# Four heads at a time through a block-causal attention in front of a two-layer network

## The chip, the cores and the metric

The kernel runs on one core of one Trainium2 chip, in one launch. The core has a matrix engine (TensorE; PE in the profile, its weight loads PEld), a vector engine (VectorE, DVE), a scalar engine (ScalarE, ACT), a general engine (GpSimd, POOL) and a sync engine (SyncE, SP) whose queue issues nearly all transfers. The metric is device time in microseconds. Times of one kernel are given as the median of several runs; a profile is one execution.

## The reference

The attention has 8 batches of 8 heads, 576 positions and 64 values per head. A query sees all keys of its own block of 64 positions and of earlier blocks. Its output is laid out as 4608 tokens of 512 values and goes through a network with a hidden layer of 2048 and a leaky activation with one slope per hidden unit. Everything is float32.

```python
scores = scale * np.matmul(q, k.transpose(0, 1, 3, 2))       # scale = 1/8
mask = block_i >= block_j                                    # blocks of 64 positions, 9 of them
scores = np.where(mask, scores, -1000000000.0)
scores = scores - np.max(scores, axis=-1, keepdims=True)
attn = np.exp(scores)
attn = attn / (np.sum(attn, axis=-1, keepdims=True) + 1e-09)
out = np.matmul(attn, v)
x = out.transpose(0, 2, 1, 3).reshape(B * S, H * D)
h = x @ w_in
g = np.maximum(h, 0.0) + alpha * np.minimum(h, 0.0)
y = g @ w_out
```

## The kernel before

The work has two stages that overlap. In the first, the attention runs pair of heads by pair of heads (32 pairs), and beside it the part of the network that belongs to the first 6 of 16 hidden blocks (`FA`) is computed for chunks of 256 tokens (`chunk_a`, 18 chunks: `ffn1` at L501, `activate`, `ffn2` at L540). Its results go to memory (`part`). In the second stage the other 10 hidden blocks are computed for chunks of 512 tokens (`pair1`, L581, with fewer products by a Strassen scheme, and `ffn2`), and the partial sums are added. Weights arrive as 64-bit numbers and are made float32 by seven instructions (`to_f32`, 512 columns at a time, a "piece"), and each operand of the dense products is split into a rounded high part and a low part (`split`).

All instructions are given to a planner (`Plan`) with a cost and a priority. The planner simulates the engines greedily and writes out one order for each engine; on the chip each engine runs its order and waits where data are late. What the simulation takes as cost (`c_tiled` and others) decides only about order. Buffers are taken by the planner too: three "duos" (two PSUM banks each) serve the attention, two more banks the dense products.

One pair of heads in the attention has these steps. Score products (`scores`, L722, K=64 rows by 32 columns of weights) put a block of 64 queries onto 128 partitions, `32*i`: `i // 2` chooses the half of the queries and `i % 2` the half of each key block, so that one query's keys lie in two partition rows and one query block `T` needs `32 * (T + 1)` columns. The blocks of a pair go in three sets: TOP (8, 6), MID (7, 5), LOW (4 to 0). DVE takes row maxima (L727), POOL exchanges them between the two rows of a query (`swap`, L699, four copies), DVE combines them (L730), ACT takes exponentials and row sums (L735, an activation and a reading of the accumulator each), and DVE transposes 32x32 blocks (L739) into `PTL` (query blocks 0 to 3) and `PTH` (4 to 8). `factors_of` exchanges the sums (L699 again), inverts them (L750) and spreads them over the partitions (L756 on ACT, L758 on DVE). `values` (L780, 64x64 products) multiplies with the values: for each key block `j`, two heads `h` and two query halves `g`, with all query blocks that see it as columns. One instruction of DVE (L786) multiplies by the inverse sums and writes `xT`, a ring for two batches in SBUF. A float32 matmul that the kernel writes appears in the trace as two matmul records.

The first four query blocks of a batch are computed a batch ahead of the others (`SKEW`): the four pairs of batch 0 start with FIRST (3 to 0) alone, and the last four pairs have no LOW set but THEN (4,). After each batch `spill` writes its part of `xT` to memory (`xd`) for the second stage, and `chunk_x` takes 256 tokens from the ring, splits them and starts a chunk; `tail_x` collects the last 64 tokens of four batches. Four weight pieces of the second stage are converted during the attention and stored (`AHEAD`, `weights_ahead`, `wd`); the others are converted when the attention has ended.

Of the kernel before, what the change touches and what calls it, by code (L numbers as in the profile page):

```python
# [29 lines left out]
RING = 2 * S  # L30
# [9 lines left out]
LAG = 6.25  # L40
VL = 1.0
E0, E1 = -5, 1
NEAR = 20
FP = -1
AHEAD = {(8 + k // 2, k % 2): 12 + 4 * k for k in range(4)}
# [5 lines left out]
RB, EB, EF = 2, 3, 4  # L51
LO_A = ("POOL", "POOL")
QA, VA = 3, 3
PB, QB, VB, TB, CB = 5, 3, 3, 2, 6
SWAP = "POOL"
RCP = ("ACT", "ACT", "ACT", "ACT")
PM, PX, PT, PZ, PU = -7, -8, -1, -1, -10
GH, XH, XC = ("ACT", "POOL"), "ACT", 2
LATER = ("DVE", "POOL", "DVE", "POOL", "DVE", "DVE")
# [5 lines left out]
TO_POOL = 85  # L65


IN_ORDER = {"q", "k", "v", "p", "PTL", "PTH", "z", "r", "R", "raw", "m", "ef", "xb", "X", "xt", "qa", "va", "tail"}
# [16 lines left out]
class Plan:  # L85
# [44 lines left out]
    def schedule(self):  # L130
# [43 lines left out]
        while events:  # L174
# [13 lines left out]
            for engine, heap in ready.items():  # L188
# [29 lines left out]
                if engine == "PE":  # L218
                    saved = SWITCH if before and before.tiled and cost.tiled else 0.0
                    before = cost  # L220
                    cost = clock(t, cost) - saved
                elif engine in ("DVE", "ACT", "POOL"):
                    cost *= LONGER
# [31 lines left out]
    def issue(self):  # L255
        for _, i in self.schedule():
            self.ops[i][2]()

# [42 lines left out]
def attn_ffn(ctx, tc, qT, kT, vT, w_in, w_out, alpha, out):  # L301
# [26 lines left out]
    xT = xring.tile([P, NCC, RING], F32, name="xT")  # L328
# [12 lines left out]
    def rooms(pool, *kinds):  # L341
        for kind, n, shape, dt in kinds:
# [4 lines left out]
    rooms(st, ("q", QB, [S - CHA], F32), ("qa", QA, [2, CHA], F32), ("va", VA, [4, 2, D], F32), ("k", QB, [S], F32), ("v", VB, [NT, 2, D], F32), ("p", PB, [1024], F32),  # L347
          ("PTL", TB, [1024], F32), ("PTH", TB, [2880], F32), ("c", CB, [3, 10], F32), ("z", 2, [3, 2 * NT], F32),
          ("r", 2, [2, NT], F32), ("R", 2, [2, 32 * NT], F32))
    rooms(xring, ("tail", 1, [NCC, CHA], F32), ("xh", XC, [NCC, CHA], F32R), ("xl", XC, [NCC, CHA], F32R))  # L350
# [15 lines left out]
    def to_f32(src, prio, after=(), early=None):  # L366
# [17 lines left out]
        op("DVE", 350, lambda: nc.vector.tensor_scalar(  # L384
# [4 lines left out]
        op("DVE", 390, lambda: nc.vector.tensor_scalar(  # L389
            out=fr(), in0=high(), scalar1=0xFFFFF, scalar2=0x100000, op0=ALU.bitwise_and, op1=ALU.bitwise_or),  # L390
            r=[raw], w=[eb], prio=prio)
        op("DVE", 760, lambda: nc.vector.scalar_tensor_tensor(  # L392
# [3 lines left out]
        op("DVE", 680, lambda: nc.vector.scalar_tensor_tensor(  # L396
# [5 lines left out]
    def split(src, hi, lo, n, r, hk, lk, claim, on, prio):  # L402

        op("ACT", c_act(n, True), lambda: nc.scalar.copy(out=hi(), in_=src()), r=r, w=[hk], claim=claim, prio=prio)  # L404
        op(on, c_pool(n) + 60 if on == "POOL" else 1.4 * c_dve(n), lambda: (nc.gpsimd if on == "POOL" else nc.vector).tensor_tensor(  # L405
            out=lo(), in0=src(), in1=hi().bitcast(F32), op=ALU.subtract), r=[*r, hk], w=[lk], claim=claim, prio=prio)
# [12 lines left out]
    def add(e, n, to, a, b, f, prio, r=()):  # L419

        op(e, c_pool(n) if e == "POOL" else 1.3 * c_dve(n), lambda: (nc.gpsimd if e == "POOL" else nc.vector).tensor_tensor(
# [4 lines left out]
    def weights_ahead(p):  # L426

        for f, i in (k for k in AHEAD if AHEAD[k] == p):
            pr = 5 * p + 100
            mb, _ = to_f32((w_in, w_out)[i][f].bitcast(I32), pr, [("x", p // NP % 2, p % NP, 1)])  # L430
# [116 lines left out]
    def factors(t0):  # L547
# [3 lines left out]
           r=["att", *[("xd", b, i) for b in range(t0 // S, (t0 + CHB - 1) // S + 1) for i in range(2)]], w=[xb], prio=0 if t0 else XB)  # L551
# [76 lines left out]
    def chunk_x(b, part, s0):  # L628

        xh, xl = Buf("xh"), Buf("xl")  # L630
        r0 = b % 2 * S + s0
        split_x(lambda: xT[:, :, r0:r0 + CHA], xh, xl, slice(0, CHA), xs(b, (part,)), 0, FP, CHA)
        return xh, xl, [0]

    tails = {}

    def tail_x(b):

        i = b % (CHA // 64)
# [18 lines left out]
    def blocks(ap, n, j0):  # L658

        return ap[:, :64 * n].rearrange("p (j x) -> p j x", x=64)[:, :, j0:j0 + 32]  # L660

    def prep(p, pr):

        q, k, v = Buf("q"), Buf("k"), Buf("v")
        op("SP", 160, lambda: nc.sync.dma_start(out=q(), in_=qT[p, :, CHA:]), w=[q], prio=pr)
        op("SP", 288, lambda: nc.sync.dma_start(out=k(), in_=kT[p]), w=[k], prio=pr)
        op("SP", 576, lambda: nc.sync.dma_start(out=v(), in_=vT[p]), w=[v], prio=pr + VL)
        return (lambda: q(), lambda: k(), CHA, [q, k]), v

    def prep_first(p, pr):  # L670

        qk, v = Buf("qa"), Buf("va")
        for i, src in enumerate((qT, kT)):
            queue, issuer = (("SP", nc.sync), ("ACTQ", nc.scalar))[i and not p]
            op(queue, 128, lambda i=i, src=src, issuer=issuer: issuer.dma_start(out=qk()[:, i], in_=src[p, :, :CHA]), w=[(qk, i)], prio=pr)
        op("SP", 256, lambda: nc.sync.dma_start(out=v(), in_=vT[p, :, :4]), w=[v], prio=pr + VL)
        return (lambda: qk()[:, 0], lambda: qk()[:, 1], 0, [(qk, 0), (qk, 1)]), v

    def at_T(T):

        u = T - 4 if T > 3 else T
        return 32 * u * (18 if T > 3 else 8)

    def run_of(T, T1, h, j):

        u, step = (T - 4, 18 + h) if T > 3 else (T, 8 + h)
        start = step * u + h * (5 if T > 3 else 1) + j
        return start, step, T1 - T

    def swap(t, to, of, n, keys, key, scale, pr):  # L690

        cost = {"DVE": 75, "POOL": 258, "ACT": 150}[SWAP]

        def move(a, b):
            o, i = t()[a, to, n], t()[b, of, n]
            if SWAP == "ACT":
                nc.scalar.activation(out=o, in_=i, func=AF.Copy, scale=scale)
            else:
                (nc.vector if SWAP == "DVE" else nc.gpsimd).tensor_scalar(out=o, in0=i, scalar1=scale, scalar2=None, op0=ALU.mult)  # L699
        for i in range(4):  # L700
            a, b = slice(32 * i, 32 * i + 32), slice(32 * (i ^ 1), 32 * (i ^ 1) + 32)
            op(SWAP, cost, lambda a=a, b=b: move(a, b), r=keys, w=[(*key, i)], prio=pr)
        return [*keys, *[(*key, i) for i in range(4)]]

    def scores(src, Ts, pts, z, pr):

        sb, pb, c = Buf("duo"), Buf("p"), Buf("c")
        n = 2 * len(Ts)
        off, at = {}, 0
        for T in Ts:  # L710
            off[T] = at
            at += 32 * (T + 1)

        def qk_run():
            for T in Ts:
                w = 32 * (T + 1)
                q, k, q0, _ = src[T > 3]
                for i in range(4):
                    for h in range(2):
                        at = 64 * T - q0 + 32 * (i // 2)  # L720
                        hs, qs = slice(64 * h, 64 * h + 64), slice(at, at + 32)
# [207 lines left out]
```

## Time and profile before

| | |
|---|---|
| median of 3 runs | 1066.98 us (1065.96 to 1069.24) |
| the profiled execution | 1068.6 us, its span 1066.8 us |
| PE busy | 1013.9 us, 95% |
| DVE, ACT, POOL busy | 766.7, 590.7, 581.7 us |
| mean granted TensorE clock | 0.979 of full speed |
| DMA | 119.56 MB, 112 GB/s on average |

Views used below: the page gives busy shares; a table of stretches gives for each engine the busy microseconds and, in brackets, the number of instructions; a timeline gives start, length, engine, line, tiles and count of merged instructions, and in square brackets the idle time before them with what ended it ("issue": nothing that the profile shows). A group of instructions has, after the bar, busy time, mean nanoseconds of one, idle time before and its releaser.

### The profile page before, as it was taken

What the parts mean: (1) busy time and instruction counts of PE and PEld (TensorE: products, weight loads), DVE (VectorE), ACT (ScalarE), POOL (GpSimd) and SP (SyncE); (2) the same over time, 40 slices, a digit from 0 to 9 for tenths busy, and PEclk for the clock granted to TensorE, in tenths of its full rate; (3) what the DMA queues carried; (4) which work ended last, traced back from release to release, by engine and by line L of the source; (5) the groups of instructions that cost most, each with busy time, mean ns of one, the idle gap of its engine ahead of it and who ended that gap; (6) DMA issues with size and microseconds to landing.
All of it is one profiled execution on the core that took longest, in us unless ns stands there. A gap on an engine that the chain in (4) does not pass through costs nothing.

```text
span 1066.8 us, 32551 instructions
## 1 busy us (share of the span) xinstructions
PE 1013.9 (95%) x12860; PEld 876.9 (82%) x12860; DVE 766.7 (72%) x1674; ACT 590.7 (55%) x2106; POOL 581.7 (55%) x1036
## 2 busy tenths in 40 slices
PE   6667999999999999999998999999999999999998
PEld 4445888888888888888776879898989889898987
DVE  6899888878788877875889986656565556565552
ACT  6776868677766756865555553434343434343431
POOL 4778645564654654666999682525252525252521
PEclk9768999999999999999999999999999999999999
DMA  8534554453646354330633122121212121212021
GB/s 293 191 123 148 187 195 140 150 175 131 206 151 209 98 184 151 103 121 25 204 119 124 55 80 80 40 79 41 80 40 80 41 80 40 80 41 79 2 80 40
DMA packets 66890, 119.56 MB, mean 112 GB/s; under 512 B 10288, under 2 KB 31024, under 8 KB 66736
## 3 DMA queue, kind: packets, MB, share of 16 engines
q1 hardware_dynamic: 66304, 117.20, 33.1%
q8 instruction: 101, 1.65, 0.7%
q14 instruction: 53, 0.43, 0.1%
q10 hardware_dynamic: 432, 0.27, 0.1%
HBM read 87.04 MB, written 29.36 MB: 109 GB/s over the span
## 4 chain that ended last, share of the span: by engine, by line
PE 83%; DVE 6%; POOL 5%; issue 3%; ACT 3%; DMA 0%; SPq 0%; DVEq 0%; POOLq 0%; ACTq 0%
PE bank L540 34%; PE bank L581 19%; PE bank L501 14%; PE duo L722 8%; PE duo L780 8%; ACT p L735 2%; POOL gl L523 2%; POOL c L699 1%; DVE g L514 1%; DVE c L727 1%; DVE m L396 1%; DVE m L384 1%; DVE ef L389 1%; DVE ef L392 1%; DVE bank L594 0%
## 5 line engine op out<-in xcount | busy, mean ns | idle before, releaser
L523 POOL TENSOR_TENSOR gl<-g,gh 128x256 fp32r<-128x256 f32 x288 | 232.6, 811 | 284.1 <-ACT gh L520 268.7
L581 PEld LDWEIGHTS bank<-X,w 128*128 128x128 f32 x1890 | 254.4, 189 | 27.5 <-DVE X L405 2.7
L581 PE MATMUL bank<-X,w 128*128 128x256 f32 x1890 | 261.3, 282 | 7.0 <-DVE X L405 2.2
L735 ACT ACTIVATE p<-duo,c 128x256 f32<-128x256 f32 (+8 forms) x576 | 220.2, 413 | 47.1 <-DVE c L730 46.6
L540 PE MATMUL bank<-w,gh 128*128 128x512 f32 x720 | 225.4, 394 | 0.0
L512 ACT ACTIVATE g<-bank 128x256 f32<-128x256 f32 x288 | 109.0, 386 | 143.0 <-DVE bank L594 93.4
L514 DVE SCALAR_TENSOR_TENSOR g<-g,oal,bank 128x256 f32<-128x256 f32 x288 | 134.0, 474 | 42.5 <-ACT g L512 38.3
L520 ACT CAST gh<-g 128x256 fp32r<-128x256 f32 x234 | 94.6, 407 | 123.9 <-PE bank L540 98.3
L699 POOL TENSOR_SCALAR c<-c 32x4 f32<-32x4 f32 (+3 forms) x400 | 99.7, 249 | 100.9 <-DVE c L727 69.8
L594 DVE TENSOR_TENSOR bank<-bank,g 128x256 f32<-128x256 f32 x180 | 74.8, 427 | 109.8 <-PE bank L581 108.9
L540 PE MATMUL bank<-wa,gh 128*128 128x512 f32 x432 | 142.5, 410 | 8.9 <-ACT wa L404 3.2
L540 PE MATMUL bank<-w,gl 128*128 128x512 f32 x360 | 141.9, 394 | 0.0
L727 DVE TENSOR_REDUCE c<-duo 128x2 f32<-128x512 f32 (+8 forms) x288 | 123.8, 478 | 18.0 <-PE duo L722 17.6
L540 PEld LDWEIGHTS bank<-w,gh 128*128 128x128 f32 x720 | 121.2, 188 | 13.6
L735 ACT ACTIVATION_READ_ACCUMULATOR p<-duo,c 128x1 f32 x576 | 129.7, 225 | 0.0
L501 PE MATMUL bank<-xh,wa 128*128 128x256 f32 x864 | 127.6, 289 | 0.3 <-POOL wa L405 0.2
L501 PEld LDWEIGHTS bank<-xh,wa 128*128 128x128 f32 x864 | 113.6, 192 | 11.2 <-issue 6.1
L739 DVE STREAM_TRANSPOSE PTH<-p 128x576 f32<-128x576 f32 (+4 forms) x160 | 99.5, 630 | 16.2 <-ACT p L735 14.4
L540 PEld LDWEIGHTS bank<-wa,gh 128*128 128x128 f32 x432 | 78.1, 191 | 32.5 <-issue 5.6
L722 PE MATMUL duo<-k,q 64*32 64x288 f32 (+4 forms) x2560 | 85.1, 377 | 12.4 <-ACT p L735 12.3
L540 PE MATMUL bank<-wa,gl 128*128 128x512 f32 x216 | 88.0, 408 | 5.7 <-POOL gl L523 5.6
L590 DVE TENSOR_TENSOR g<-bank,g 128x256 f32<-128x256 f32 x135 | 55.9, 419 | 39.3 <-PE bank L581 39.2
(66 smaller groups left out, 1350.8 us busy)
## 6 DMA issues: line engine op xcount, KB each, us to landing
v<-in_v SPq DMA_DIRECT2D x32, 576.0 KB, 3.9
k<-in_k SPq DMA_DIRECT2D x32, 288.0 KB, 4.7
xb<-xd SPq DMA_DIRECT2D x9, 1024.0 KB, 5.4
m<-part SPq DMA_DIRECT2D x36, 256.0 KB, 3.5
out<-m SPq DMA_DIRECT2D x35, 256.0 KB, 2.0
va<-in_v SPq DMA_DIRECT2D x32, 256.0 KB, 4.5
raw<-in_w_in SPq DMA_DIRECT2D x16, 512.0 KB, 3.9
raw<-in_w_out SPq DMA_DIRECT2D x16, 512.0 KB, 3.5
```

What stands on the lines that cost most here:

```text
L501: nc.tensor.matmul(hp()[:, :n], ww()[:, 0, cc * P:(cc + 1) * P], x()[:, cc, :n], start=(i == 0 and cc == 0), stop=(i == 2 and cc == NCC - 1))
L512: op("ACT", c_act(CHA), lambda: nc.scalar.activation(out=g(), in_=hp()[:, ts], func=AF.Relu, scale=-1.0), r=[hp], w=[g], prio=FP)
L514: op("DVE", c_dve(CHA) + 60, lambda: nc.vector.scalar_tensor_tensor(out=g(), in0=g(), scalar=oal[:, f:f + 1], in1=hp()[:, ts], op0=ALU.mul ...
L520: op("ACT", c_act(CHA, True), lambda: nc.scalar.copy(out=gh(), in_=g()), r=[g], w=[gh], prio=FP)
L523: op("POOL", c_pool(CHA) + 60, lambda: nc.gpsimd.tensor_tensor(out=gl(), in0=g(), in1=gh().bitcast(F32), op=ALU.subtract), r=[g, gh], w=[g ...
L540: nc.tensor.matmul(acc(), a()[:, ts], ww(), start=(first and i == 0), stop=(last and i == 2))
L581: nc.tensor.matmul(bank()[:, :CHA], W()[:, i, 256 * at + P * c:256 * at + P * c + P], B()[:, j, CHA * c:CHA * c + CHA], start=(n == 0), st ...
L699: (nc.vector if SWAP == "DVE" else nc.gpsimd).tensor_scalar(out=o, in0=i, scalar1=scale, scalar2=None, op0=ALU.mult)
L722: nc.tensor.matmul(sb()[32 * i:32 * i + 32, h, off[T]:off[T] + w], q()[hs, qs], blocks(k()[hs], T + 1, 32 * (i % 2)), start=True, stop=True)
L727: op("DVE", c_dve(2 * w), lambda t=t, w=w, o=o: nc.vector.tensor_reduce(out=c()[:, 0, 2 * t:2 * t + 2], in_=sb()[:, :, o:o + w], axis=AX.X ...
L735: op("ACT", 237 + w / 1.2, lambda x=2 * t + h, T=T, h=h, w=w, o=o: nc.scalar.activation(out=pb()[:, 2 * o + h * w:2 * o + h * w + w], in_= ...
L739: op("DVE", 85 + 2.08 * w, lambda to=to, a=a, w=w, o=o: nc.vector.transpose(out=to()[:, a:a + 2 * w], in_=pb()[:, 2 * o:2 * o + 2 * w]), r ...
```

## The change

Four heads (two pairs) go through the attention together. The partition group `32*i` now holds pair `i // 2` and query half `i % 2`, so all keys of a query lie in one row, a query block needs `64 * (T + 1)` columns, and maxima and sums need no exchange: `swap` is gone. Block 8 has 576 columns and is cut into 512 and 64; its smaller maximum is taken from both cuts, and its sums are added. The three sets of two pairs become six sets of four heads. The transposed blocks now have 32 keys on the partitions of each pair and query half, so `values` multiplies 32 rows by 64 columns of weights: 32-key blocks `j` (two per key block), two heads `h` and four partition groups `i`, for three groups of query blocks (0 to 3, 4 to 6, 7 and 8) instead of two, into two duos at once.

x has no ring any more. The product with the inverse sums goes into a small tile `xo` for each pair and from there to memory at once; each chunk (`chunk_again`) loads its 256 tokens from `xd` again, all but the first chunk, which is taken from SBUF. The inverse sums are spread by 16 copies instead of 4, half on POOL and half on ACT. Sixteen weight pieces instead of four are converted ahead. The `gh` casts of the chunks all go to POOL, the low parts of later weights all to DVE, and most priorities and buffer numbers, and some of the costs that the planner uses, are set anew. q, k and v are loaded for four heads at once.

```diff
-TOP, MID, LOW = (8, 6), (7, 5), (4, 3, 2, 1, 0)
-FIRST, THEN = (3, 2, 1, 0), (4,)
+NQ = NPAIR // 2
+NB = NP // 2
+WHOLE = {T: (T, 0, 2 * T + 2) for T in range(NT)}
+LONG = ((8, 0, 16),), ((8, 16, 18), WHOLE[6]), (WHOLE[7],)
+BOTH = *LONG, (WHOLE[5], WHOLE[1]), (WHOLE[4], WHOLE[2]), (WHOLE[3], WHOLE[0])
+LAST = *LONG, (WHOLE[5],), (WHOLE[4],)
+FIRST = (WHOLE[3], WHOLE[2]), (WHOLE[1], WHOLE[0])
+GROUPS = (0, 4, 12, 52), (4, 7, 24, 76), (7, 9, 32, 68)
-C0, C1 = -3, 1.5
+C0, C1 = -3, 3.5
-AHEAD = {(8 + k // 2, k % 2): 12 + 4 * k for k in range(4)}
+AHEAD = {(8, 0): 3, (8, 1): 3, (9, 0): 4, ... (15, 0): 13, (15, 1): 14}
-GH, XH, XC = ("ACT", "POOL"), "ACT", 2
-LATER = ("DVE", "POOL", "DVE", "POOL", "DVE", "DVE")
+GH, XH, XC = ("POOL",), "ACT", 2
+LATER = ("DVE", "DVE", "DVE", "DVE", "DVE", "DVE")
...
+    def chunk_again(parts):
+        x = Buf("xc")
+        n = CHA // len(parts)
+        for i, (b, part, s0) in enumerate(parts):
+            op("SP", 2 * n, lambda i=i, b=b, s0=s0: nc.sync.dma_start(out=x()[:, :, n * i:n * i + n], in_=xd[:, :, b * S + s0:b * S + s0 + n]),
+               r=[("xd", b, part, pair) for pair in range(NP)], w=[(x, i)], prio=FP)
+        return chunk_x(x, [(x, i) for i in range(len(parts))])
...
     def scores(src, sets, pts, z, pr):
+                for (T, a, e), w, o in zip(items, ws, offs):
+                    q, k, q0, _ = src[T > 3]
+                    for i in range(4):
+                        for h in range(2):
+                            at = 64 * T - q0 + 32 * (i % 2)
+                            hs = slice(64 * h, 64 * h + 64)
+                            nc.tensor.matmul(sb()[32 * i:32 * i + 32, h, o:o + w], q()[hs, i // 2, at:at + 32], k()[hs, i // 2, 32 * a:32 * e],
+                                             start=True, stop=True)
...
     def factors_of(z, T0, T1, pr):
-        keys = swap(z, 1, 0, ns, ...)
+        for i in range(4):
+            for b in range(4):
+                to, of = slice(32 * b, 32 * b + 32), slice(32 * i, 32 * i + 32)
+                on = RCP[(i + b) % 2]                       # "POOL", "ACT"
...
     def values(u, vs, pts, R, parts, pr, to=None):
+        obs = [Buf("duo") for a in range(2)]
+        groups = [g for g in (0, 1, 2) if (g > 0) in parts]
         def run():
-            for i, (a, e) in zip(parts, ranges):
-                for j in range(e):
-                    T = max(j, a)
+            for g in groups:
+                a, e, base, _ = GROUPS[g]
+                v = vs[g > 0]
+                for j in range(2 * e):
+                    T = max(j // 2, a)
                     for h in range(2):
-                        for g in range(2):
-                            gs = slice(64 * g, 64 * g + 64)
-                            nc.tensor.matmul(ob()[64 * h:64 * h + 64, g, 32 * T:32 * e], v[i]()[gs, j, h, :], x, start=(j == 0), stop=(j == e - 1))
+                        for i in range(4):
+                            gs = slice(32 * i, 32 * i + 32)
+                            x = pts[g]()[gs]
+                            x = bass.AP(x.tensor, x.offset + 32 * place(T, h, j), [x.ap[0], [32 * (base + 2 * h), e - T], [1, 32]])
+                            nc.tensor.matmul(obs[i // 2]()[64 * h:64 * h + 64, i % 2, 32 * T:32 * e], v()[gs, j, h, :], x, start=(j == 0), stop=(j == 2 * e - 1))
...
+            for i in () if to else parts:
+                s0, s1 = ((0, CHA), (CHA, S))[i]
+                of = b if i else b + SKEW
+                op("SP", (s1 - s0) / 2, lambda of=of, s0=s0, s1=s1, xo=xo, pair=pair: nc.sync.dma_start(
+                    out=xd[:, pair, of * S + s0:of * S + s1], in_=xo()[:, s0:s1]), r=[(xo, pair)], w=[("xd", of, i, pair)], prio=FP)
```

More of the change, by code (lines that the diff above doesn't have):

```diff
@@ L222, in schedule @@
                 elif engine in ("DVE", "ACT", "POOL"):
-                    cost *= LONGER
+                    over = min(1.0, max(0.0, busy.get("POOL", 0.0) - t) / cost) * BESIDE if isinstance(cost, Beside) else 0.0
+                    cost = cost * LONGER + over
                 lat = LAT.get(engine, 0)
@@ L677, in prep_first @@
         return (lambda: qk()[:, 0], lambda: qk()[:, 1], 0, [(qk, 0), (qk, 1)]), v
[L679 to L703, printed above, removed]
@@ new lines, in exponents, with move @@
+    def exponents(sb, pb, z, pts, what, pr):
+        for t, ((T, a, e), w, o, (c, m, x)) in enumerate(what):
+            for h in range(2):
+                zi = 2 * (T if not a else NT) + h
+                op("ACT", 237 + w / 1.2, lambda x=x, h=h, w=w, o=o, c=c, zi=zi: nc.scalar.activation(
+                    out=pb()[:, 2 * o + h * w:2 * o + h * w + w], in_=sb()[:, h, o:o + w], func=AF.Exp, bias=c()[:, 1, x + h:x + h + 1], scale=0.125,
+                    accum_out=z()[:, 0, zi:zi + 1]), r=[sb, (c, m)], w=[(pb, t, h), (z, "s", zi)], prio=pr + PX)
+            to, at, n = pts[group_of(T)], 32 * place(T, 0, 0), 64 * (T + 1)
+            def move(to=to, at=at, n=n, a=a, w=w, o=o):
+                nc.vector.transpose(out=to()[:, at:at + 2 * n].rearrange("p (h x) -> p h x", h=2)[:, :, 32 * a:32 * a + w],
+                                    in_=pb()[:, 2 * o:2 * o + 2 * w].rearrange("p (h x) -> p h x", h=2))
+            op("DVE", 85 + 2.08 * w, move, r=[(pb, t, 0), (pb, t, 1)], w=[(to, T, a)], prio=pr + PT)
@@ L817, in attn_ffn @@
-    for p in range(NPAIR):
-        pr, of = p * 5, p + SKEW * NP
-        b = p // NP
-        both = of < NPAIR
-        src, v = prep(p, pr - 4.5)
-        srcs, vs, pts, parts = (None, src), (None, v), (None, Buf("PTH")), (1,)
+    for u in range(SKEW * NB):
+        pr = 2 * E1 * (u - SKEW * NB) + E0
+        if not u % NB:
+            xs = Buf("xc")
+        src, v = prep_first(u, pr - 4 * E1)
+        pts, z = (Buf("PTL"), None, None), Buf("z")
+        scores((src,), FIRST, pts, z, pr)
+        values(u - SKEW * NB, (v,), pts, factors_of(z, 0, 4, pr), (0,), pr + E1 + .5, xs)
+        if u % NB == NB - 1:
+            of = u // NB
+            op("SP", 512, lambda xs=xs, of=of: nc.sync.dma_start(out=xd[:, :, of * S:of * S + CHA], in_=xs()),
+               r=[(xs, pair) for pair in range(NP)], w=[("xd", of, 0, pair) for pair in range(NP)], prio=pr + 20)
+            chunk(chunk_x(xs, [(xs, pair) for pair in range(NP)]), [of * S + P * t for t in range(CHA // P)])
@@ L826, in attn_ffn @@
         z = Buf("z")
[L827 to L841 removed]
+        scores(srcs, BOTH if both else LAST, pts, z, pr)
@@ new lines, in attn_ffn @@
+        R = factors_of(z, 0 if both else 4, NT, pr + SF)
+        values(u, vs, pts, R, parts, pr + SV)
+        weights_ahead(u)
+        if u % NB == NB - 1:
+            chunk(chunk_again([(b, 1, CHA)]), [b * S + CHA + P * t for t in range(CHA // P)])
+            if b + SKEW < B:
+                chunk(chunk_again([(b + SKEW, 0, 0)]), [(b + SKEW) * S + P * t for t in range(CHA // P)])
+            if b % 4 == 3:
+                last = range(b - 3, b + 1)
+                chunk(chunk_again([(i, 1, S - 64) for i in last]), [i * S + S - 64 for i in last])
```

263 lines of the change are left out of this document (115 added, 148 removed).

## The prediction

> **What bounds the kernel now.** I read the page first (busy shares), then four stretches of the span, then PE's timeline inside the attention.
>
> ```profile
> span 1066.8 us, 32551 instructions
> PE 1013.9 (95%) x12860; PEld 876.9 (82%) x12860; DVE 766.7 (72%) x1674; ACT 590.7 (55%) x2106; POOL 581.7 (55%) x1036
> ```
>
> ```profile
> core 0: us, PE busy (x) PEld busy (x) DVE busy (x) ACT busy (x) POOL busy (x), PEclk, DMA share, GB/s
> 0.00:106.70 106.70, 72.16 (x1557) 54.15 (x1557) 91.99 (x219) 73.67 (x299) 74.25 (x147) 0.81 0.57 189
> 106.70:500.00 393.30, 391.54 (x7862) 334.05 (x7861) 312.65 (x762) 281.30 (x1235) 225.50 (x590) 1.00 0.46 150
> 500.00:680.00 180.00, 167.04 (x1081) 145.45 (x1080) 147.73 (x235) 93.22 (x214) 136.70 (x132) 0.99 0.30 99
> 680.00:1066.80 386.80, 383.13 (x2367) 343.29 (x2365) 214.34 (x462) 142.49 (x360) 145.22 (x168) 1.00 0.17 58
> ```
>
> PE is the bound. Up to 106.7 us it idles 34.5 us while DVE is 86% busy: the start belongs to DVE. From 106.7 to 500 us PE idles 1.8 us, so a microsecond added to PE's attention work there is a microsecond of time, and one taken from ACT, DVE or POOL is worth nothing. From 500 to 680 us PE idles 13 us, with DVE at 82% and POOL at 76%. After 680 us the change touches nothing.
>
> **What PE does in the attention.** A pair of heads in the steady part, as PE's timeline has it:
>
> ```profile
> 219.25 0.82 PE L780 MATMUL duo<-PTL,va 64*64 64x128 f32 x32
> 219.89 2.15 PE L780 MATMUL duo<-PTH,v 64*64 64x160 f32 x72
> 221.97 0.50 PE L722 MATMUL duo<-k,q 64*32 64x160 f32 x16
> 222.27 0.92 PE L722 MATMUL duo<-qa 64*32 64x128 f32 x64
> 223.12 0.75 PE L501 MATMUL bank<-xh,wa 128*128 128x256 f32 x4
> 227.15 1.85 PE L722 MATMUL duo<-k,q 64*32 64x288 f32 x64
> 228.94 1.21 PE L501 MATMUL bank<-xh,wa 128*128 128x256 f32 x8
> ```
>
> From start to start, a value product takes 2.72 us (219.25 to 221.97) for 104 matmul records: `values` writes 52 matmuls, so each is two records and, by the equal counts of PE and PEld, two weight loads, four instructions. The LOW scores take 1.15 us for 80 records, TOP and MID together 1.79 us for 64.
>
> **Value products, the decisive term.** The new `values` writes, for four heads, 8 matmuls for each 32-key block of three groups of 8, 14 and 18 blocks: 320 matmuls, so 640 records and 640 loads, 1280 instructions in one uninterrupted run. The two operations that it replaces have 416. Streamed columns are 2880 for four heads as now (2 x 1440), so by columns it would cost 2 x 2.72 = 5.44 us, no change. The question is whether PE gets 1280 instructions in 5.4 us, 4.3 ns each. The busiest part now, values plus LOW, is 368 instructions in 3.87 us, 10.5 ns each, and it already breaks at times:
>
> ```profile
> 113.81 0.92 PE L722 MATMUL duo<-qa 64*32 64x128 f32 x64
> 114.66 0.82 PE L780 MATMUL duo<-PTL,va 64*64 64x128 f32 x32
> 115.30 1.99 PE L780 MATMUL duo<-PTH,v 64*64 64x160 f32 x57
> 117.88 0.43 PE L780 MATMUL duo<-PTH,v 64*64 64x64 f32 x15 [0.60 <-issue]
> ...
> 433.84 2.16 PE L780 MATMUL duo<-PTH,v 64*64 64x160 f32 x72
> 435.93 0.50 PE L722 MATMUL duo<-k,q 64*32 64x160 f32 x16
> 436.22 0.81 PE L722 MATMUL duo<-qa 64*32 64x128 f32 x50
> 437.31 0.29 PE L722 MATMUL duo<-qa 64*32 64x32 f32 x14 [0.28 <-issue]
> ```
>
> ```profile
> 339.37 0.80 PE L722 MATMUL duo<-qa 64*32 64x128 f32 x51 [0.34 <-issue]
> ```
>
> Three times PE stops in the middle of one operation, waiting for nothing that the profile shows. Instructions come in packets of their own, and the stops lie a whole number of packets apart:
>
> ```profile
> q8 instruction: 101, 1.65, 0.7%
> 117.88:339.36 221.48, 221.15 (x4712) 1.00 0.51 167
> 339.36:437.31 97.95, 97.63 (x1912) 1.00 0.44 139
> ```
>
> 25,720 PE and PEld instructions in 101 packets are 255 each: a page of 256. Between the stops lie 2 x 4712 = 9424 and 2 x 1912 = 3824 instructions, 48 and 16 short of 37 and 15 pages, which semaphore instructions, not listed, can fill. So I read them as page boundaries at which the next page had not arrived. Its price: 256 instructions, 128 matmuls, before the first stop is matmul 25 of the 64 begun at 113.81, that is 114.14 us; the page began at 117.88, 3.74 us later. Before the third stop, 66 matmuls back to 435.93 and 62 more end at matmul 10 of the 72 begun at 433.84, 434.13 us: 3.18 us. If a page is asked for when the one before it is entered, PE gets a page each 3.2 to 3.7 us at best; I take 3.5, the middle.
>
> The new operation crosses five boundaries. The first page after its start was asked for earlier; the other four wait: 4 x 3.5, and the 256 instructions outside these intervals at 4.3 ns, 1.1 us: 15.1 us against 5.44, +9.7. Fourteen full operations give +135. The last two have no first part (1024 instructions, 3 x 3.5 + 1.1 = 11.6, against two of 72 records, 219.89 to 221.97, 2.1 us each): +7.4 each, +15. The two FIRST ones (256 instructions, one boundary) cost nothing. Together +150; at the start PE has idle time, so I let one operation's +10 hide: **+140**. With 3.18 us the same working gives +8.4 x 14 + 6.4 x 2 = 130, with 3.74 it gives +10.6 x 14 + 8.1 x 2 = 165.
>
> The Trainium skill's "Runtime: NRT & Kernel Launch", section "Instruction fetch mechanics", says that the cost of crossing a 16 KiB boundary is "mostly hidden". By that rule the value products would stay at 5.4 us, as in the first rival below. The three stops speak against it here.
>
> **Clock.** A run in which PE works 1.1 us of each 3.5 looks like this stretch:
>
> ```profile
> 526.70:530.10 3.40, 1.38 (x5) 0.63 (x5) 3.37 (x5) 1.68 (x4) 3.40 (x5) 1.00 0.30 77
> 530.10:533.50 3.40, 3.40 (x9) 2.63 (x10) 2.79 (x4) 1.24 (x2) 3.40 (x4) 0.51 0.00 0
> ```
>
> 1.38 us busy in 3.4, and the next 3.4 us ran at 0.51. Waiting itself loses nothing by it, but the dense products after each value operation would run half fast for one such stretch, losing 1.7 us: 14 x 1.7 = **+24** (bounds 0, and two stretches, 48).
>
> **Scores.** Twice the keys in a row and half the rows: the same columns (2880 for four heads), 160 records instead of 288, six sets as now. Before, 2 x (1.15 + 1.79) = 5.9 us for 2 x 144 records; TOP and MID show 1.79 us for 960 columns without issue trouble, which makes 2880 columns 5.4 us. -0.5 x 16 = **-8**. Its 320 instructions in 5.4 us are 17 ns each, slower than a page needs.
>
> **The start.** DVE's work up to 107 us, and the fixed part of one instruction:
>
> ```profile
> L727 DVE TENSOR_REDUCE c<-duo 128x2 f32<-128x256 f32 (+8 forms) x63 | 24.9, 437 | 5.0 <-PE duo L722 5.0
> L739 DVE STREAM_TRANSPOSE PTH<-p 128x576 f32<-128x576 f32 (+4 forms) x20 | 12.0, 620 | 0.0
> L739 DVE STREAM_TRANSPOSE PTL<-p 128x256 f32<-128x256 f32 (+3 forms) x32 | 9.0, 313 | 0.8 <-ACT p L735 0.7
> L727 DVE TENSOR_REDUCE c<-duo 128x2 f32<-128x576 f32 x32 | 23.6, 738 | 3.3 <-PE duo L722 3.3
> L727 DVE TENSOR_REDUCE c<-duo 128x2 f32<-128x64 f32 x32 | 6.8, 213 | 0.0
> ```
>
> 512 elements make 525 ns, so 148 ns of a reduction are fixed; a transpose's is taken as the same. Half of 63 reductions and of 52 transposes go: 57 x 0.148 = 8.4 us, with some of the small bias and sum steps about **-11**. The POOL copies of maxima and sums go too; exponentials fall from 18 for a pair, 576, to 320 (14 x 20 + 2 x 12 + 2 x 8), which spares ACT off the path. Bounds: 0 (weights are now converted at later priorities) to -20.
>
> **The change-over.** Twelve more weight pieces are converted during the attention, so two of fourteen remain in this stretch:
>
> ```profile
> L392 DVE SCALAR_TENSOR_TENSOR ef<-raw,ef 128x512 int32<-128x512 int32 x14 | 17.4, 1242 | 0.0
> ```
>
> ```profile
> PE bank L540 <- POOL gl L523: 5.6, 7, 1.5
> PE bank L581 <- DVE X L405: 2.2, 2, 1.3
> ```
>
> Of the 13 us idle I give back **-8** (0 to -13): the waits for X and w and part of those for gl, where POOL, beside the conversions, is late. The low halves that move from POOL to DVE there have DVE's freed time (17.4 us for one of four conversion steps) as cover.
>
> **Costed at nothing.**
>
> ```profile
> L699 POOL TENSOR_SCALAR c<-c 32x4 f32<-32x4 f32 (+3 forms) x400 | 99.7, 249 | 100.9 <-DVE c L727 69.8
> xb<-xd SPq DMA_DIRECT2D x9, 1024.0 KB, 5.4
> ```
>
> ```profile
> xd<-xT SPq DMA_DIRECT2D x8, 512.0 KB, 5.9
> ```
>
> POOL loses the 99.7 us of bias copies, and gains 8 small copies at 0.25 us for each of 18 factor steps (36 us), half of the chunks' casts `gh` (54 of 108), and the products of twelve weight pieces. x goes out for each pair and comes back before each chunk but the first: a write (5.9 us now) and a read (5.4), on SP's queue, which gets half as many q, k, v loads. The conversions moved into the attention, with one `wd` write and one read each on SP's queue, run beside PE on a DVE at 79% (312.65 of 393.3). A chunk starts some 11 us later; what hides it is the backlog of dense products, which alone fill PE after 500 us. Should that cover fail, PE would wait up to 11 us at a chunk. A value product takes two of the three duos, so one score set is held back meanwhile: PE runs in order and is in the value product anyway.
>
> **Sum.** 140 + 24 - 8 - 11 - 8 = +137 us on the profiled execution's 1068.6 us (span 1066.8; the median of the runs is 1066.98, 0.15% lower): **1205 us**. Ends: 130, two operations hidden (-20), -8, -20, -13, no clock loss: +69, 1138; 165 + 48 - 8 = +205, 1274 at the worst.
>
> **Rivals.** (1) *Pages are no limit* (deeper ahead than the stops suggest): values 5.4 to 5.9 us, no clock loss, and 1068.6 - 8 - 11 - 8 + 16 x 0.25 = 1046 us, faster. For it: only three stops beside 28 full value products, of 0.3 to 0.6 us. Against: values and LOW are 1.4 pages, so a late page shows only where two boundaries fall within them. It decides from a page price below 1.1 us, a third of the smallest read. (2) *Pages bind, but half as hard*: a page each 2.2 us where the memory queues are quiet; 4 x 2.2 + 1.1 = 9.9, +4.5 x 14 + 3.5 x 2 = 70, less the same 27 and with half the clock loss: 1124 us. For it speaks nothing but that each of the three pages was read under a busy memory (DMA share 0.44 and 0.51 in the rows above). (3) *The wait spreads to DVE*: every engine runs a written order, and the product that ends `values` (L786) stands in DVE's. DVE then waits some 10 us, and behind it the next sets' reductions and transposes, for which ACT and then PE wait. If a set's two reductions and transposes (0.74 us each by the longest row), 3 us, come out on top after each of 14 operations, it is 1205 + 42 = 1247 us. Against it: dense products are there to fill PE.
>
> **How the numbers follow.** Forecast, 1205 us, 0.72, rival 1 0.15, rival 2 0.07, rival 3 0.06. Faster by over 0.3% (what this measurement can tell from no change) is rival 1, 0.15, slower 0.83, between them 0.02 for gains and losses that cancel. The range goes from 1095, below rival 2, to 1260, above rival 3; it leaves out rival 1 and the far ends.
>
> **What would show it.** In the profile after: some 138 instruction packets (12,860 records less 3,328 and 4,608, plus 10,240 and 2,560 by the code, twice, by 256); PE's timeline with `values` as runs of about 128 records broken by "issue" idle time of 2 us or more; about 14 to 16 us for one; a granted clock below 1 in the slices of the attention; a chain with more "issue"; POOL without L699; DVE idle for PE. Unbroken value products of 5 to 6 us would prove me wrong.

## The result, and the profile after

The changed kernel takes 1254.8 us (median; 1251.77 to 1257.21) beside 1068.0 us for the kernel before on the same chip: ratio 1.175, interval 1.1715 to 1.1784. The profiled execution took 1257.21 us, with a span of 1255.3. The page of the changed kernel, its shares, PE's and the granted clock's slices, the queue that brings instructions, and the chain that ended last by engine:

```profile
span 1255.3 us, 41084 instructions
PE 1096.0 (87%) x17724; PEld 917.7 (73%) x17724; DVE 724.6 (58%) x1406; ACT 510.9 (41%) x1540; POOL 478.7 (38%) x680
...
PE   5756777977987797897787999999999999999998
...
PEclk9786986878979797987898899999999999999999
...
q8 instruction: 139, 2.28, 0.8%
...
PE 78%; issue 11%; DVE 5%; ACT 3%; POOL 2%; DMA 1%; ACTq 0%; DVEq 0%; POOLq 0%
```

The last 18 slices are a PE that is at least 80% busy, nearly all of them 90% or more, at a clock near full. In the first 22 slices PE is mostly 50 to 90% busy, and the clock dips in the same slices. DVE has less work than before and is 58% busy. Two groups of the page say who waits for whom (after the bar: busy us, mean ns of one, idle us before and its releaser):

```profile
L788 PE MATMUL duo<-PT,v 32*64 32x64 f32 (+1 forms) x8192 | 134.2, 285 | 114.2 <-issue 114.2
...
L798 DVE TENSOR_TENSOR xo<-duo,R 128x576 f32<-128x576 f32 (+1 forms) x32 | 21.7, 719 | 190.6 <-PE duo L788 190.6
```

PE sat idle for 114.2 us inside these value products, waiting for nothing that the profile shows ("issue"), and DVE sat for 190.6 us behind that. With the products of the first group of query blocks (`PTL`), PE's idle time of this kind is 117.8 us in 62 stops:

```profile
PE duo L788 <- issue: 117.8, 62, 4.2
```

PE's timeline shows one value product from its second boundary on, and the dense products behind it:

```profile
302.67 1.69 PE L788 MATMUL duo<-PT,v 32*64 32x96 f32 x128 [2.37 <-issue]
306.67 2.26 PE L788 MATMUL duo<-PT,v 32*64 32x64 f32 x128 [2.32 <-issue]
310.67 2.20 PE L788 MATMUL duo<-PT,v 32*64 32x64 f32 x128 [1.75 <-issue]
314.40 0.44 PE L788 MATMUL duo<-PT,v 32*64 32x32 f32 x8 [1.53 <-issue]
314.77 2.08 PE L514 MATMUL bank<-xh,wa 128*128 128x256 f32 x8
```

Each run has 128 records, 256 instructions with their weight loads, and 4.00, 4.00 and 3.73 us lie from one start to the next. From its first record to the next product the operation takes 17.8 us (from 297.0 us); the fourteen full ones take 16.1 to 19.9 us, 244.2 us together, 17.4 each, where the two operations that one replaces took 5.44. The last two take 13.3 and 15.0 us.

The attention as a stretch, to the last record of the value products, first before and then after (engine columns as in the stretches of the prediction):

```profile
0.00:504.20 504.20, 467.91 (x9506) 392.26 (x9506) 406.51 (x982) 356.70 (x1538) 302.32 (x742) 0.96 0.48 157
```

```profile
0.00:693.60 693.60, 542.35 (x14310) 424.77 (x14313) 398.79 (x744) 291.16 (x999) 222.74 (x389) 0.83 0.42 138
```

The attention grew by 189.4 us, the span by 188.5. Of the 189.4, PE's busy time has 74.4 (542.35 - 467.91) and its idle time 115.0 (151.2 against 36.3). What follows the attention takes 561.7 us against 562.6: PE's idle time there falls by 8.5 us (16.6 to 8.1), but its busy time rises by 7.7 (546.0 to 553.6), since dense products that ran beside the attention now run behind it.

### The profile page after: what moved, and what is told of

Its sections match the earlier page's. It is cut to its first block, busy times and chain, and to the rows that moved or that the text cites. A ratio compares the mean times of both kernels' runs of the same rounds, so it can differ in the third digit from the quotient of the medians.

```text
span 1255.3 us, 41084 instructions
## 1 busy us (share of the span) xinstructions
PE 1096.0 (87%) x17724; PEld 917.7 (73%) x17724; DVE 724.6 (58%) x1406; ACT 510.9 (41%) x1540; POOL 478.7 (38%) x680
## 3 DMA queue, kind: packets, MB, share of 16 engines
q8 instruction: 139, 2.28, 0.8%
## 4 chain that ended last, share of the span: by engine, by line
PE 78%; issue 11%; DVE 5%; ACT 3%; POOL 2%; DMA 1%; ACTq 0%; DVEq 0%; POOLq 0%
PE bank L553 30%; PE bank L594 17%; PE duo L788 13%; PE bank L514 12%; PE duo L707 7%; ACT p L735 2%; DVE c L712 1%; POOL gl L536 1%; DVE PT L741 1%; DVE g L527 1%; POOL ws L434 0%; ACT r L761 0%; DVE w L418 0%; DMA qa<-in_k 0%; DVE PTL L741 0%
## 5 line engine op out<-in xcount | busy, mean ns | idle before, releaser
L788 PE MATMUL duo<-PT,v 32*64 32x64 f32 (+1 forms) x8192 | 134.2, 285 | 114.2 <-issue 114.2
L553 PE MATMUL bank<-w,gh 128*128 128x512 f32 x720 | 225.4, 394 | 0.0
L788 PEld LDWEIGHTS duo<-PT,v 32*64 32x64 f32 x8192 | 121.8, 170 | 125.1 <-issue 124.6
L735 ACT ACTIVATE p<-duo,c 128x64 f32<-128x64 f32 (+7 forms) x320 | 156.7, 509 | 73.9 <-DVE c L718 42.6
L531 POOL CAST gh<-g 128x256 fp32r<-128x256 f32 x108 | 47.4, 441 | 290.7 <-DVE g L527 154.5
L553 PE MATMUL bank<-wa,gh 128*128 128x512 f32 x432 | 144.4, 415 | 3.4 <-POOL wa L418 2.7
L514 PEld LDWEIGHTS bank<-xh,wa 128*128 128x128 f32 x864 | 121.0, 204 | 30.7 <-issue 11.0
L553 PE MATMUL bank<-w,gl 128*128 128x512 f32 x360 | 141.9, 394 | 0.0
L798 DVE TENSOR_TENSOR xo<-duo,R 128x576 f32<-128x576 f32 (+1 forms) x32 | 21.7, 719 | 190.6 <-PE duo L788 190.6
L553 PEld LDWEIGHTS bank<-w,gh 128*128 128x128 f32 x720 | 120.7, 188 | 12.9
L712 DVE TENSOR_REDUCE c<-duo 128x2 f32<-128x128 f32 (+7 forms) x160 | 113.3, 745 | 24.3 <-PE duo L707 23.7
L533 ACT CAST gh<-g 128x256 fp32r<-128x256 f32 x180 | 72.8, 406 | 107.9 <-PE bank L553 95.4
L707 PE MATMUL duo<-k,q 64*32 64x512 f32 (+4 forms) x1536 | 91.7, 561 | 14.3 <-ACT p L735 14.0
L553 PEld LDWEIGHTS bank<-wa,gh 128*128 128x128 f32 x432 | 80.3, 195 | 30.7 <-issue 10.0
L741 DVE STREAM_TRANSPOSE PT<-p 128x1024 f32<-128x1024 f32 (+2 forms) x96 | 88.5, 939 | 10.0 <-ACT p L735 9.7
```

Of the source, the lines that this page charges most:

```text
L514: nc.tensor.matmul(hp()[:, :n], ww()[:, 0, cc * P:(cc + 1) * P], x()[:, cc, :n], start=(i == 0 and cc == 0), stop=(i == 2 and cc == NCC - 1))
L553: nc.tensor.matmul(acc(), a()[:, ts], ww(), start=(first and i == 0), stop=(last and i == 2))
L707: nc.tensor.matmul(sb()[32 * i:32 * i + 32, h, o:o + w], q()[hs, i // 2, at:at + 32], k()[hs, i // 2, 32 * a:32 * e], start=True, stop=True)
L712: op("DVE", c_dve(2 * w), lambda t=t, w=w, o=o, sb=sb, c=c: nc.vector.tensor_reduce(out=c()[:, 0, 2 * t:2 * t + 2], in_=sb()[:, :, o:o + w ...
L735: op("ACT", 237 + w / 1.2, lambda x=x, h=h, w=w, o=o, c=c, zi=zi: nc.scalar.activation(out=pb()[:, 2 * o + h * w:2 * o + h * w + w], in_=s ...
L741: nc.vector.transpose(out=to()[:, at:at + 2 * n].rearrange("p (h x) -> p h x", h=2)[:, :, 32 * a:32 * a + w], in_=pb()[:, 2 * o:2 * o + 2 ...
```

## The experiments

The theory after the result: a page of 256 PE instructions arrives every 3.5 to 4.0 us, and a value product that asks for them faster stops at each boundary. Rivals: the 32x64 shape itself is slow, or four heads at once wait on the chain through ACT and DVE, and the stops are only where that shows.

**Value product in pieces.** The same instructions, cut into operations of at most 256, which the planner sets 2.4 us apart, so that it puts dense products between them:

```diff
+        slices = [steps[i:i + 8] for i in range(0, len(steps), 8)]
+        for n, part in enumerate(slices):
+            op("PE", c_tiled(cols, 8 * len(part)), lambda part=part: run(part), ..., w=[*obs, (obs[0], "part", n)], prio=pr)
+            if n + 1 < len(slices):
+                op("GAP", 2400, lambda: None, r=[(obs[0], "part", n)], w=[(obs[0], "gap", n)], prio=pr)
```

> The changed kernel with the value products of four heads cut into five operations of 256 instructions (128 matmul records) each, with room for at least 2.4 us of other work between two of them in the planner's order; nothing else changed, same products. Page theory (256 instructions arrive no faster than every 3.5 to 4 us): the stops inside value products nearly vanish, since dense products fill the time in which a page is fetched; value products take about 7 us of PE for four heads instead of 17, the granted clock goes back to nearly 1; 1060 to 1110 us. Rival, the shape (products of 32 rows by 64 columns, or their two duos, are slow in themselves): each slice takes its fifth of 17 us, 3.4 us, and the time stays at 1240 us or rises with the switches.

Measured: 1173.38 us, ratio 1.0995 (1.0977 to 1.1013). Three pieces in PE's timeline with a few of the products between them, then PE's waits over the whole span (us in total, times, longest):

```profile
300.10 1.73 PE L789 MATMUL duo<-PT,v 32*64 32x96 f32 x128
...
304.35 1.59 PE L789 MATMUL duo<-PT,v 32*64 32x64 f32 x128
305.87 1.22 PE L514 MATMUL bank<-xh,wa 128*128 128x256 f32 x8
...
308.93 1.57 PE L789 MATMUL duo<-PT,v 32*64 32x64 f32 x128
```

```profile
PE duo L707 <- ACT p L735: 23.8, 14, 4.6
PE duo L789 <- ACT p L735: 16.1, 11, 2.3
PE duo L789 <- issue: 14.0, 13, 3.6
```

The stops fall from 117.8 us to 14.0 with the same instructions, shape and data: they come from asking for pages too fast, and the kernel is 81 us faster. The eight dense records that took 2.08 us behind the unbroken operation take 1.22 here: that was the clock. But the time misses the expected 1060 to 1110. A piece of 128 records takes 1.6 to 1.8 us, not the 1.1 that the columns ask for; the five pieces of an operation take 8.1 us at a full clock against 5.44. PE's busy time in the value products is 154.0 us against 96.8 before, 57 more. At a full clock and without a stop the number of instructions costs 42 of them (14 x (8.1 - 5.44) = 37, and 2.1 for each of the last two operations, 6.36 in four pieces against 4.22); the other 15 I put down to the 26 of the 80 pieces that ran at a lower clock or had a stop in them. The remainder of the 106 us is idle time: 82.0 us in the attention against 36.3, much of it for ACT's exponents, as the first two rows say.

**Fewer instructions, first try.** Query blocks 4 to 8 as one group: 208 matmuls for 320, 832 instructions for 1280. The larger `PT` needs room, taken from other buffers:

```diff
-GROUPS = (0, 4, 12, 52), (4, 7, 24, 76), (7, 9, 32, 68)
+GROUPS = (0, 4, 12, 52), (4, 9, 32, 164)
-RB, EB, EF = 2, 4, 4
+RB, EB, EF = 2, 3, 4
-PB, QB, VB, TB, TL, CB, RR = 4, 2, 1, 3, 2, 6, 1
+PB, QB, VB, TB, TL, CB, RR = 3, 2, 1, 2, 2, 6, 1
-GB = 6
+GB = 5
```

> The changed kernel with query blocks 4 to 8 as one group instead of two (4 to 6, 7 and 8): the same columns and the same shape, but 208 matmuls and 832 instructions for four heads instead of 320 and 1280. To make room, three p and m buffers instead of four and five gh and gl instead of six. Page theory: 3.25 pages, so about 2.25 x 3.75 + 1.1 = 9.5 us for a value product instead of 17.4; 14 x 7.9 + 2 x 8 = 127 us less and some clock regained: 1110 to 1140 us. Shape theory by columns: no change, 1250. Cost by matmul without pages: 0.65 x 17.4 = 11.3 us, some 1155 us, without stops at page boundaries.

Measured: 1243.65 us, ratio 1.1659 (1.1636 to 1.1682). The fourteen full value products fell to 10.9 us on average, where 9.5 was expected; the time hardly fell. The second stage of the dense products (L553) by stretches of the attention in this kernel:

```profile
100.00:200.00 100.00, 1.24 (x3) 0.48 (x3) 0.81 0.52 175
200.00:300.00 100.00, 0.00 (x0) 0.00 (x0) 0.81 0.52 178
300.00:400.00 100.00, 0.00 (x0) 0.00 (x0) 0.80 0.49 171
```

None ran from 200 to 400 us, where the changed kernel has 90 and 87 in each 100. A chunk needs its six `gh` and `gl` at once while only one accumulator is there, and I had left five (`GB`): the dense products that should fill PE came late, most of them after the attention. The experiment was flawed and says nothing on the theory beyond the length of the operation.

**Fewer instructions, with six buffers.** The same with `GB` left at 6 and `EF` at 3:

> The changed kernel with groups 4-6 and 7-8 joined again (208 matmuls, 832 PE instructions per value operation in place of 288 and 1152), the six gh/gl buffers kept (the room comes from p, m and ef: three buffers each). Page theory: the value operation takes 9.5 to 12.1 us as in the first try of this (one to three stops of 1.7 to 2.5 us), 6 to 7 us less than the changed kernel, in 14 operations, and a little less in the other two: 1135 to 1160 us, with FFN2 rows in every 100 us of the attention (the first try had none from 200 to 300 us). Rival (the stops are not what costs; the attention of four heads is bound by its chain over ACT and DVE): 1230 us or more, like the first try.

The changed kernel has 320 matmuls and 1280 instructions in an operation, not the 288 and 1152 of this expectation; its times do not hang on them. Measured: 1124.08 us, ratio 1.0515 (1.0486 to 1.0545), 131 us less than the changed kernel and below even the range expected. Here is a value product of it, and the page's group:

```profile
362.66 1.85 PE L788 MATMUL duo<-PT,v 32*64 32x160 f32 x88
365.52 2.28 PE L788 MATMUL duo<-PT,v 32*64 32x160 f32 x128 [1.01 <-issue]
368.97 0.96 PE L788 MATMUL duo<-PT,v 32*64 32x96 f32 x68 [1.17 <-issue]
```

```profile
L788 PE MATMUL duo<-PT,v 32*64 32x160 f32 (+4 forms) x4608 | 85.4, 282 | 41.6 <-issue 41.6
```

From stop to stop it is again 3.45 us (365.52 to 368.97), with 128 records; but wider products use up more of it (2.28 us), and there are one to three stops in an operation instead of three to five. The fourteen full operations take 8.8 to 13.0 us, 9.95 on average. 14 x (17.4 - 9.95) = 104 us, and the last two (6.9 and 6.6 us) give another 15. The other 12 of the 131 are not traced to a cause; the mean clock rose from 0.906 to 0.974.

**Both.** Joined groups in four pieces:

> The joined groups and the value operation cut into four pieces of at most 256 instructions with 2.4 us between them. Page theory: no stop over 1 us inside a piece, the four pieces together 6 to 7 us (208/288 of the 8.1 us of the five pieces without the joining), 16 x 2 us less than the cut kernel's 1173 us, so 1125 to 1150 us; it stays above the kernel before because the pieces still have 832 instructions against 2 x 180 and because the matrix engine waits for ACT's exponents more often. Rival (what is left over the kernel before in the cut kernel is waiting, not instructions): 1165 to 1180 us, unchanged.

Here too the share is 208/320 and not 208/288, which makes 5.3 us of the 8.1. Measured: 1095.19 us, ratio 1.0241 (1.0219 to 1.0262), again below the range. The four pieces take 6.5 us at a full clock (1.74, 2.38, 1.97 and 0.39 from start to next start): the wider products take longer for each record. The attention of this kernel, and the value products alone in it:

```profile
0.00:550.80 550.80, 499.31 (x10823) 382.66 (x10827) 407.46 (x752) 297.55 (x1009) 226.86 (x401) 0.96 0.52 175
```

```profile
0.00:550.80 550.80, 116.96 (x6651) 104.86 (x6655) 0.96 0.52 175
```

The attention is 46.6 us longer than before. 20.1 are the value products (116.96 against 96.84 busy), 15.2 more idle time (51.5 against 36.3; PE waits 12.9 us for ACT's exponents before value products); and the other 11 are dense products, less 3 for the scores: 24 FFN1 and 18 FFN2 matmul records more run here and not behind the attention (some 8 us at 0.138 and 0.273 us each). What is behind the attention takes 19.0 us less than before (543.6 against 562.6): PE's busy time there is 10.1 us less, for those products, and its idle time 8.9 less (16.6 to 7.8), which fits the conversions. Of every way tried, the four-head layout stays slower than the pairs.

**The kernel before, with narrow products.** If the count is the cause, the old layout must suffer from it too. In the kernel before, every value matmul is written for 32 columns at a time: 180 matmuls for a pair instead of 52, the same 64x64 weights, the same columns in all:

```diff
-                for j in range(e):
-                    T = max(j, a)
+                for T, j in ((T, j) for T in range(a, e) for j in range(T + 1)):
```

> The kernel before, with each value product written as products of 32 columns, one for each query block that sees a key block: the same columns and the same 64x64 shape, but 180 matmuls and 720 instructions for a pair instead of 52 and 208. Page theory: 2.8 pages, (2.8 - 1) x 3.75 + 1.8 = 8.6 us instead of 2.7, stops at page boundaries, a lower clock in the attention: 1230 to 1290 us. If pages are no limit: 90 waves of four products at 57 ns by the weight loads, 5.1 us, no stops: about 1145 us.

Measured: 1294.61 us, ratio 1.2112 (1.2059 to 1.2164), just above the range. A value product in its timeline (before: 104 records in 2.72 us):

```profile
313.65 1.37 PE L779 MATMUL duo<-PTL,va 64*64 64x32 f32 x80
314.83 1.81 PE L779 MATMUL duo<-PTH,v 64*64 64x32 f32 x110
317.70 2.07 PE L779 MATMUL duo<-PTH,v 64*64 64x32 f32 x128 [1.06 <-issue]
321.16 0.88 PE L779 MATMUL duo<-PTH,v 64*64 64x32 f32 x42 [1.39 <-issue]
```

Again 128 records between stops, 3.46 us from start to start. The shape 32x64 is not needed for it, nor is the four-head chain; both rivals fall as the main cause of the stops.

**A page's price by itself.** The kernel before with 1100 tiny bf16 products at its start, 32 columns of weights and 16 moving, that nothing waits for:

```diff
+    for _ in range(1100):
+        nc.tensor.matmul(bank[:32, :16], warm[:, :32], warm[:, :16], start=True, stop=True)
```

> The kernel before with 1100 tiny bf16 matmuls (32 weight columns, 16 moving columns, no tiling of rows, result unused) right after the warm-up ones, 2200 instructions, 8.6 pages, while little else runs. Page theory: stops after every 128 matmuls, 3.4 to 3.8 us from page to page, some 30 us in all. If the stops belong to the tiled float32 products: an even run of these matmuls without stops, 10 to 28 us.

Measured: 1102.0 us in a single run, and this timeline at the start:

```profile
3.33 5.85 PE L363 MATMUL bank<-warm 128*32 128x16 bf16 x213
12.14 7.02 PE L363 MATMUL bank<-warm 128*32 128x16 bf16 x256 [2.96 <-issue]
19.32 3.56 PE L363 MATMUL bank<-warm 128*32 128x16 bf16 x128 [0.17 <-issue]
23.05 3.56 PE L363 MATMUL bank<-warm 128*32 128x16 bf16 x128 [0.17 <-issue]
27.05 3.56 PE L363 MATMUL bank<-warm 128*32 128x16 bf16 x128 [0.44 <-issue]
```

These products go one by one, 27.4 ns each (7.02 us for 256), so that a page lasts 3.56 us by itself, and the stops left over are small: starts 3.73 and 4.00 us apart, where 3.4 to 3.8 was expected. Some boundaries show none: the 256 from 12.14 us and the last 247 ran through. Where there are stops they lie 128 products apart here too, and the price is the same before the attention has begun. It doesn't tell how much faster a page could come if products were shorter.

**The conversions alone.** The kernel before with 16 instead of 4 weight pieces converted in the attention (`AHEAD` in order of the changed kernel, spread over pairs 6 to 29):

> The kernel before with one part of the change alone: 16 in place of 4 weight pieces are converted during the attention. The prediction's term: the idle matrix engine at the change-over falls from 13 to about 5 us and nothing is paid in the attention: 1057 to 1061 us. Rival A (the 12 more pieces cost the attention as much, on DVE, POOL or the queues): 1064 to 1070 us. Rival B (they delay the attention's own chain by more): over 1072 us.

Measured: 1060.05 us, ratio 0.9916 (0.9901 to 0.993). The stretch behind the attention, before and then in this kernel, and its attention:

```profile
504.20:680.00 175.80, 162.84 (x1005) 141.38 (x996) 145.86 (x231) 91.48 (x208) 134.12 (x128) 0.99 0.31 101
```

```profile
0.00:507.80 507.80, 470.10 (x9506) 392.11 (x9506) 424.56 (x1026) 367.69 (x1561) 325.40 (x751) 0.97 0.53 174
507.80:680.00 172.20, 166.75 (x1058) 147.68 (x1047) 109.93 (x198) 81.92 (x194) 113.87 (x123) 1.00 0.29 92
```

The attention pays 3.6 us, and PE's idle time behind it falls from 13.0 to 5.4 us; DVE's busy share there falls from 83 to 64%. This part of the change is a gain, and this kernel is faster than both.

**The conversions undone in the kernel with pieces.** `AHEAD` cut to four pieces:

```diff
-AHEAD = {(8, 0): 3, (8, 1): 3, (9, 0): 4, ... (15, 1): 14}
+AHEAD = {(8, 0): 6, (8, 1): 8, (9, 0): 10, (9, 1): 12}
```

> The cut kernel (five pieces per value operation) with only 4 of the 16 weight pieces converted during the attention: this undoes the conversions alone. If they are worth in the changed kernel what they are worth in the kernel before (8 us), 1179 to 1184 us against the cut kernel's 1173 us. Rival: in the changed kernel the attention is longer and waits more, so that twelve conversions fewer on DVE and ACT shorten it by as much: 1169 to 1176 us.

Measured: 1188.07 us, ratio 1.1108 (1.1087 to 1.1129), against 1.0995 with sixteen. So the conversions are worth 0.0113 x 1068 = 12 us there (some 9 to 15 by the two intervals together), where 6 to 11 was expected. The attention has the same length without them (629.7 us and 630.2 us), so here they cost it nothing.

**The last part that can be moved over.** The kernel before with the sixteen pieces and `LATER` all on DVE:

> The kernel before with the 16 pieces converted during the attention and, as in the change, all the later splittings of the weights on DVE. Both theories price the second part: if the idle 3 us from 507.8 to 560 and the 2.5 us from 560 to 640 us of the matrix engine are POOL's (48.2 of 52.2 us busy there), 1056 to 1059 us; if not, 1059 to 1062 us, as with the 16 pieces alone.

Measured: 1060.43 us, ratio 0.9919 (0.9902 to 0.9935), the same as without it. So POOL, busy for most of that stretch, was not what PE waited for there, as far as this exchange tells: the work only went from POOL to DVE.

## Why the prediction was right, point by point

**The page as the limit.** Right, and shown: the stops go when the same instructions are spread (1173 us), shrink when there are fewer (1124), and come to the kernel before when it gets more (1295). The count of packets, 138 predicted, is 139. The packets of the instruction queue in the changed kernel's trace show the wait itself. Each of the 62 stops ends 1.2 to 1.6 us after a packet of 16 KB has landed (median 1.4); the packet took 1.0 us (median); and the next one starts 1.04 us at the least (median 1.1) after PE has gone on. The three medians add up to about 3.5 us, near the least period measured (3.454). In all 45 stretches of 128 records between two stops exactly one packet started and landed: the next page is on its way only when the one before it has been entered.

The Trainium skill's "Runtime: NRT & Kernel Launch", section "Instruction fetch mechanics", has the boundary "mostly hidden". Here it costs 118 us of idle PE; in the kernel before, with 28 full products, the prediction's timelines had three stops of 0.28 to 0.60 us.

The second rival (a page each 2.2 us where the memory queues are quiet) falls too. In the operation shown, the only DMA packets that started between 302 and 315 us are three of instructions, and the pages still lay 4.00 and 3.73 us apart:

```profile
306.00:310.00 4.00, 2.26 (x128) 2.07 (x128) 0.00 (x0) 0.00 (x0) 0.00 (x0) 0.50 0.02 4
310.00:314.77 4.77, 2.57 (x136) 2.37 (x136) 0.00 (x0) 0.00 (x0) 0.00 (x0) 0.50 0.02 3
```

**The size of the value term.** Mis-sized: 150 us before hiding against 187 measured (14 x (17.4 - 5.44) = 167, and 28.3 for the last two against 4 x 2.1, 20), outside the 130 to 165 that I had given as its ends. The page costs 3.73 us by the median of 45 periods, 3.45 at the least, where I took 3.5 out of 3.18 to 3.74. The part outside the four waits is 17.4 - 4 x 3.73 = 2.5 us, where I took 1.1: that came from pricing 256 instructions by streamed columns at 4.3 ns each, and 128 records take 1.6 to 1.8 us at a full clock even where no page is late (the pieces above). I let one operation hide in the start; none did.

The same slip was in the first rival. With pages no limit at all the value products would have cost 42 us more (the pieces at a full clock) and not 4, so 1046 - 4 + 42 = 1084 us by that working, and not faster. By this estimate no price of a page leads to a gain.

**The clock.** The sign and place were right: half clock behind each value product. By the mean granted clock 0.906 x 1255.3 us against 0.979 x 1066.8 us some 236 us ran at half speed, 191 us more than before; by the losses counted next, most of that was waiting or the value products themselves. What other products lost: scores 116.8 us of busy time against 109.0 in the joined and cut kernel, and 0.143 us for each FFN1 matmul against 0.134 before, 9 us for 1020; 17 us, where I took 24.

**Scores.** Expected -8. PE's busy time in them was 112.0 us in the attention before and is 109.0 where the clock stays up (joined and cut): -3. In the changed kernel the clock makes it +5.

**The start.** Expected -11, and nothing came. PE is busy for 66.06 of the first 106.7 us against 72.16, though DVE has less to do:

```profile
0.00:106.70 106.70, 66.06 (x1875) 42.62 (x1876) 78.61 (x154) 59.04 (x203) 37.52 (x64) 0.81 0.51 178
```

PE's waits in this window, by what ended them:

```profile
PE duo L707 <- ACT p L735: 13.0, 5, 5.6
PE duo L788 <- issue: 11.6, 6, 3.6
PE duo L788 <- ACT p L735: 5.0, 4, 2.1
```

Scores and value products wait 18.0 us for ACT's exponents, and 11.6 us are stops at pages, which I had called hidden here. I had read DVE's 86% as the bound of the start, though PE's largest wait in this window was ACT's exponents in the kernel before too:

```profile
PE duo L722 <- ACT p L735: 13.1, 9, 3.0
```

With the stops nearly gone, in the joined and cut kernel, PE is busy for 70.1 us in this window, still no more than before. That ACT is the bound of the start is read from the waits and was not tested.

**The change-over.** Expected -8, of 13 us idle. In the changed kernel the stretches behind the attention show 4.6 us idle:

```profile
700.00:760.00 60.00, 57.74 (x354) 48.91 (x353) 35.28 (x50) 25.11 (x54) 50.72 (x61) 1.00 0.42 137
760.00:860.00 100.00, 97.70 (x618) 87.44 (x617) 64.41 (x133) 44.43 (x110) 49.82 (x56) 1.00 0.22 69
```

That is -8.4, and the same part in the kernel before gave a ratio of 0.9916, -9 us of 1068 (7.5 to 10.6 by the interval). The conversions in the attention, costed at nothing, cost 3.6 us there and nothing in the kernel with pieces. x from memory and the moved copies show no wait among PE's largest.

**The third rival**, DVE held up behind the value product, is in the trace (DVE waits 190.6 us for PE), but behind it PE had dense products; no 42 us for it appear in the sum, since the value products alone account for 187 of the 188.5 us.

**The sum.** Forecast 1205, profiled 1257.2. The terms that missed: value products +47 (187 for 140), scores +13, start +11, clock -15 (of 24, 9 on FFN1; its part in the scores is counted there). That makes 56 of the 52 us; the 4 us between are not traced to a term. So the mechanism was right and the decisive term a quarter too small. That the range held owes something to luck: the measured 1254.8 us lies 5 us below its upper end of 1260, and the value term by itself lay outside its own bounds.

## What to carry to other kernels

Count PE's instructions as well as its columns: a float32 product that is written once is four of them here, and a long run of which each 256 are used up in less than 3.5 to 4 us stops at nearly each page. Narrower weights (32 rows for 64) double the count for the same columns, and here a third group of query blocks made it three times the old one (1280 for 416); where they can't be avoided, join what can be joined into wider products first, and then spread the rest between long products. When several changes come as one, try the parts alone: of this one, the conversions were worth 9 us by themselves, and the rest cost 196 if the two simply add up.

## What the runs showed of the hardware

Periods from stop to stop come in steps: 3.45, 3.73 and 4.00 us, 41 of 45 in the changed kernel between 3.45 and 4.02, none below 3.454, in the kernel before with narrow products the same, and 3.73 and 4.00 with bf16. Even with their instructions there, the records of 32x64 and 32x96 float32 products start 10.6 to 11.9 ns apart (128 in 1.57 to 1.73 us with the end of the last, the wider ones hardly longer). The Trainium skill's "TensorE: Matmul & The Clock Gate", section "Wait — 56ns, not 53.3ns?", gives about 25 ns as the least from start to start: the bf16 products, which fill all rows, agree (27.4 ns), the tiled float32 ones run below it. And the clock halves without a long pause: it fell to 0.50 after a stretch of 3.41 us with 1.69 us of work, the longest pause being 2.37 us, and was still there behind the value product, where PE was full again:

```profile
301.13:304.54 3.41, 1.69 (x128) 1.54 (x128) 1.27 (x2) 0.00 (x0) 1.78 (x4) 1.00 0.03 5
304.54:307.95 3.41, 1.28 (x85) 1.28 (x89) 0.00 (x0) 0.00 (x0) 0.00 (x0) 0.50 0.03 5
314.77:318.20 3.43, 3.43 (x19) 3.43 (x17) 1.42 (x2) 0.38 (x1) 0.00 (x0) 0.50 0.61 204
```
